# P1 moved by ScalarE into the PSUM bank of P2, and four sets of operand sums moved in the program

## The chip, the cores and the metric

The kernel runs on one core of one Trainium2 chip. The metric is the device time of one execution in microseconds (us). The core has a matrix engine (TensorE, PE in the profile; its weight loads are PEld), VectorE (DVE), ScalarE (ACT), GpSimd (POOL) and SyncE (SP). Each takes its instructions in the order in which they stand; an instruction that has to wait holds up all that stand behind it on the same engine. POOL and SP mostly issue DMA transfers here. Matrix products land in PSUM, eight banks of 128 partitions x 512 fp32, and are read from there by DVE and ACT.

## The reference

```python
# q, k, v: (4, 8, 768, 64); lam: (8,)
for b in range(12):                       # blocks of 64 positions
    intra = (q_b @ k_b.T * decay_mask) @ v_b
    out_b = intra + (q_b * lam ** (pos + 1)) @ kv_state
    kv_state = lam ** 64 * kv_state + (k_b * lam ** (63 - pos)).T @ v_b
x = out.transpose(0, 2, 1, 3).reshape(3072, 512)
h = x @ w_in                              # w_in: (512, 2048)
g = h - tanh(h)
return g @ w_out                          # w_out: (2048, 512)
```

A decayed linear attention gives 3072 tokens of 512 numbers; two dense layers with `h - tanh(h)` between them give the output. All in fp32.

## The kernel before

**Tiling.** The 768 positions are cut into six groups g of 128, so that a group of all four batches has 512 tokens. For each group the kernel computes the attention, then `up` (x @ w_in, in four strips u of 512 hidden units), then `down` (g @ w_out). Attention of group g + 1 is woven between the products of group g.

**Seven products for eight.** Each dense layer is done with the scheme of Strassen and Winograd: a product of 2 x 2 blocks needs seven block products P1 to P7 instead of eight, on sums of the blocks (S1 to S4 of one side, T1 to T4 of the other), and its results are sums of products. One result block is just P1 + P2. Sums of operands are DVE instructions: `sums_in(u)` (L279, four instructions of 128x512) makes S1, S2, S3, S4 of the first weights into `ws[u]`, `att_sums` (L569 to L572) those of the tokens, `sums_out(kt)` (L285) and `sums_fine(u)` (L303) those of the second weights, which POOL's DMAs store in DRAM (`factors`, `fine`). Some products are cut again by the same scheme: `down` products 3 to 7 (`down_twice`, L858), and for groups 2 to 5 `up` products 2 and 4 (`inner_steps`, L694), whose weight sums `inner_weights(u, ns)` (L667, four instructions of 128x128 per strip and product) makes and a DMA stores in `fine_in` (L668).

**Stages.** Group 0 does `up` plainly (`up_plain`, L917), while ACT and DVE round the weights (`weights`, `round_block`, L318 to L323). Its `down` (`down_first`, L947) runs over kt = 0 to 7, seven products of two matmuls each, into seven banks; between the rounds DVE makes sums for the rounds to come: `sums_late(kt + 1)` (L956, L957) must be ready before products 6 and 3 of round kt + 1. `first_results` (L963 to L972) adds the seven banks up on DVE. Then group 1 does `up` by the seven products (`up`, L610) in the order 2, 6, 5, 7, 1 of the next strip, 4, 3. Groups 2 to 5 follow.

**P1 + P2.** In `up` of group 1, ACT copies P1 out of bank y into SBUF (L633), P2 goes to bank w, DVE adds it to the copy (L635), ACT takes tanh of the sum and DVE subtracts. In `down` of groups 1 to 5, ACT copies P1 into the tile `q1` (L811), which later sums need too, and DVE adds P2's bank to it into `o11` (L827), which is stored.

**Buffers.** `ws[u]` hold the operand sums later, but first serve as room for second weights: `pair_tiles(kt)` puts the pairs kt = 2, 3, 6, 7 into `ws[3]` with `ws[2]` or `ws[1]`, the pairs 0, 1, 4, 5 into two buffers `wt`. The pool tag "sums" has four buffers, used in turn by `inner_weights`, `sums_twice` (L837, the sums for a product that is cut again) and `inner_tokens`. A buffer of `inner_weights` is free once its store to `fine_in` has landed. POOL's DMA queue also issues the loads of second weights for `down` (`piece`, wb, L764 to L770), each when a buffer of the ring of seven becomes free by a product of PE.

**Order.** Instructions of engines stand in an order that the framework's planner makes from the program's order and its own costs; those wrapped in `keep_in_program_order` (or `tied`, `hold`) keep the order of the program among themselves.

Of the kernel before, what the change touches and what calls it, by code (L numbers as in the profile page):

```python
# [15 lines left out]
AF = mybir.ActivationFunctionType  # L16
AL = mybir.AluOpType
# [7 lines left out]
def kernel(  # L25
# [32 lines left out]
    nc = tc.nc  # L58
# [8 lines left out]
    NU = DFF // 512  # L67
    KH = KO // 2
# [139 lines left out]
    ws = [wpool.tile([128, 3, 2, 256], F32, name=f"ws_{u}") for u in range(NU)]  # L208
# [13 lines left out]
    ready = {"loaded": 0, "done": 0}  # L222
# [42 lines left out]

    def pair_tiles(kt):

        if kt % 4 > 1:
            x, y = (ws[u].rearrange("p x k c -> p (x k) c") for u in (3, 4 - kt % 4))
            return x[:, ts(kt % 4 - 2, 2)], y[:, 0:6]  # L270
        wt = wst.tile([128, 8, 256], F32, name="wt", tag="w")
        return wt[:, 0:2], wt[:, 2:8]

# [51 lines left out]
    def bank(name, tag, bufs):  # L325
        return psum.tile([128, 512], F32, name=name, tag=tag, bufs=bufs)
# [251 lines left out]
    banks, hid, blks = {}, {}, {}  # L578

    def side(g, first):  # L580

        return "zw"[first] if g < GI else "wz"[first]

    def product_bank(key, n):

        if n == 1:
            banks[key, "y"] = bank("y", "yb" if key[0] == "up" and key[2] % 2 else "ya", 1)
        if n == 5 and key[1] >= GI:
            banks[key, "z"] = bank("z", "zw"[key[2] % 2], 1)
        elif n in (2, 5):  # L590
            banks[key, "zw"[n == 2]] = bank("zw"[n == 2], side(key[1], n == 2), 1)
        t = banks[key, {2: "w", 5: "z", 3: "z"}.get(n, "y")]
        return t.rearrange("q (m c) -> q m c", m=2), n in (1, 2, 5)

    def hidden(g, c):

# [4 lines left out]
    def up(g, u, n):  # L601
        a, bname = FACT[n]
        wt = {"A11": w1[u][:, 0:2, 0], "A12": w1[u][:, 2:4, 0], "S3": w1[u][:, 0:2, 1], "A22": w1[u][:, 2:4, 1],
              "S1": ws[u][:, 0], "S2": ws[u][:, 1], "S4": ws[u][:, 2]}[a]
        x = xt[g][bname] if bname != "B11" else xt[g, 0][:, 0:2]
        key = ("up", g, u)
        t, first = product_bank(key, n)
        for m in range(2):
            for kt in range(2):
                nc.tensor.matmul(out=t[:, m, :], lhsT=wt[:, kt, ts(m, 128)], rhs=x[:, kt, :],  # L610
                                 start=first and m == 0 and kt == 0, stop=kt == 1, skip_group_check=True)

        def dst(c):
            return hidden(g, c)[:, u]

        def finish(c, src):
            th = work.tile([128, 2, HB], F32, name="th", tag="th")
            nc.scalar.activation(th, src, AF.Tanh)  # L618
            nc.vector.tensor_tensor(dst(c), src, th, op=AL.subtract)  # L619

        y, z, w = (banks[key, x].rearrange("q (m c) -> q m c", m=2) if (key, x) in banks else None for x in "yzw")
        if g >= GI and n == 1:
            nc.vector.tensor_tensor(dst(11), dst(11), y, op=AL.add)  # L623
            finish(11, dst(11))
        elif g >= GI and n == 5:
            nc.scalar.activation(dst(22), z, AF.Copy)
        elif g >= GI and n == 7:
            nc.vector.tensor_tensor(dst(22), dst(22), y, op=AL.add)
            nc.vector.tensor_tensor(dst(21), dst(21), y, op=AL.add)
            finish(22, dst(22))  # L630
            finish(21, dst(21))
        elif n == 1:
            nc.scalar.activation(dst(11), y, AF.Copy)  # L633
        elif n == 2:
            nc.vector.tensor_tensor(dst(11), dst(11), w, op=AL.add)  # L635
            finish(11, dst(11))
        elif n == 6:
            nc.scalar.activation(dst(12), y, AF.Copy)  # L638
        elif n == 7:
            nc.scalar.activation(dst(22), y, AF.Copy)  # L640
            nc.vector.tensor_tensor(dst(22), dst(22), z, op=AL.add)  # L641
            finish(22, dst(22))
        elif n == 4:
            finish(21, y)
        elif n == 3:
            nc.vector.tensor_tensor(dst(12), dst(12), z, op=AL.add)
            finish(12, dst(12))

            nc.vector.tensor_tensor(dst("S1"), dst(12), dst(22), op=AL.add)
            nc.vector.tensor_tensor(dst(12), dst(11), dst(12), op=AL.subtract)  # L650
# [3 lines left out]
    INNER = (2, 4)  # L654
# [126 lines left out]
    def otile(name):  # L781
        return opool.tile([128, 512], F32, name=name, tag="o")

    res, low = {}, {}
# [7 lines left out]
    def down(g, n):  # L792

        if n in (1, 2):
            t, first = product_bank(("down", g), n)
        else:
            t, first = bank("plain", "w" if n == 7 else "z", 1).rearrange("q (m c) -> q m c", m=2), True
        a = hidden(g, HIDAT[FACT[n][0]])
        for u in range(NU):
            wb = piece(g, n, u)  # L800
            for m in range(2):
                for kt in range(2):
                    nc.tensor.matmul(out=t[:, m, :], lhsT=a[:, u, kt, ts(m, 128)], rhs=wb[:, kt, :],  # L803
                                     start=first and u == 0 and m == 0 and kt == 0, stop=u == NU - 1 and kt == 1,
                                     skip_group_check=True)
            if u + 1 < NU:
                yield
        t = t.rearrange("q m c -> q (m c)")
        if n == 1:
            res[g, 1] = otile("q1")  # L810
            nc.scalar.activation(res[g, 1], t, AF.Copy)  # L811
        elif n == 4:
            res[g, 4] = otile("q4")
            nc.scalar.activation(res[g, 4], t, AF.Copy)
        elif n == 7:
            o = otile("q7")
            nc.vector.tensor_tensor(res[g, 4], res[g, 4], t, op=AL.add)
            store(g, 21, res[g, 4])
            nc.vector.tensor_tensor(o, res[g, 5], t, op=AL.add)
            store(g, 22, o)  # L820
        elif n == 3:
            o = otile("q3")
            nc.vector.tensor_tensor(o, res[g, 5], t, op=AL.add)
            store(g, 12, o)
        else:
            o11 = late["pool"].tile([128, 512], F32, name="o11", tag="o11", bufs=1)
            tc.keep_in_program_order(nc.vector.tensor_tensor(o11, res[g, 1], t, op=AL.add))  # L827
            store(g, 11, o11)
        yield

# [58 lines left out]
    def steps(product, n):  # L889
        for _ in range(n):  # L890
            next(product)
# [130 lines left out]
    for u, cs, n0, n1, mid, more in turns:  # L1022
        turn = up_plain(u, cs)
        if n0:
            steps(turn, KI)
            run(mid)
            weights(ready["done"] + n0)
        every(turn)
        run(more)
        weights(ready["done"] + n1)  # L1030
        if cs[-1] == 22:
            sums_first(u)
            if u == 1:
                load_weights(NU * KI)
                load(2 * B)
                powers()
            if u == 2:
                sums_in(0)
    sums_out(0)
    sums_late(0)  # L1040
    att_out(1, P1, "att")
# [3 lines left out]
    for kt in range(KH):  # L1045
        down_first(kt, (1, 2, 5, 4, 7, 6, 3) if kt + 1 < KH else (1, 2, 6, 5, 7, 3, 4))
        if kt + 1 < KH:
            sums_late(kt + 1)
        if kt + 2 < KH:
            sums_out(kt + 2)  # L1050
        if kt in (0, 1, 3, 6):
            sums_fine((kt + 1) // 2)
        if 0 < kt and kt + 3 < KH:
            weights(ready["done"] + 2)
            load_weights(ready["done"] + WAHEAD)
        if kt == 5:
            att_sums(1)
    first_results()
    sums_in(1)
    early.close()  # L1060
    late["blk"] = ctx.enter_context(tc.tile_pool(name="blk", bufs=4))
    late["pool"] = ctx.enter_context(tc.tile_pool(name="late", bufs=1))
# [20 lines left out]
    for g in range(1, NG):  # L1083
        last = g == NG - 1
        for u in range(NU):
            for n in (2, 6, 5, 7, 1, 4, 3) if g < GI else (1, 7, 3) if u == 0 else (6, 5, 1, 7, 3) if u + 1 < NU else (
                    6, 5, 7, 1, 3):
                if n != 1:
                    up(g, u, n)
                elif u + 1 < NU:  # L1090
                    up(g, u + 1, 1)
                else:
                    if g == GI - 1:
                        inner_weights(u, INNER[:1])
                        pieces(g, u)
                    every(down(g, 1))
                if g == 1 and u < 2 and n == 5:
                    sums_in(u + 2)
            if g == GI - 1:
                inner_weights(u, INNER if u + 1 < NU else INNER[1:])  # L1100
            if g >= GI or u + 1 < NU:
                pieces(g, u)
        sums_twice(g, 4)
# [72 lines left out]
```

## Time and profile before

| what | value |
|---|---|
| median of three runs | 661.0 us (659.6 to 663.91) |
| the profiled execution: its own time, its span | 661.42 us, 659.6 us |
| TensorE clock granted over the span | 1.000 |
| PE, DVE busy | 645.3 us, 486.4 us |
| ACT, POOL busy | 216.7 us, 200.6 us |
| DMA mean | 196 GB/s |

The span reaches from the first to the last instruction; the execution's own time has some 1.8 us around it. In a line of the timeline the first number is the start in us from the span's start, the second how long it took (a row with x4 merges four instructions), then engine, line, operation, written <- read tiles, and in brackets the idle time of the engine before it with what ended it. A line of waits gives the total in us, how often, and the longest.

### The profile page before, as it was taken

What the parts mean: (1) busy time and instruction counts of PE and PEld (TensorE: products, weight loads), DVE (VectorE), ACT (ScalarE), POOL (GpSimd) and SP (SyncE); (2) the same over time, 40 slices, a digit from 0 to 9 for tenths busy, and PEclk for the clock granted to TensorE, in tenths of its full rate; (3) what the DMA queues carried; (4) which work ended last, traced back from release to release, by engine and by line L of the source; (5) the groups of instructions that cost most, each with busy time, mean ns of one, the idle gap of its engine ahead of it and who ended that gap; (6) DMA issues with size and microseconds to landing.
All of it is one profiled execution on the core that took longest, in us unless ns stands there. A gap on an engine that the chain in (4) does not pass through costs nothing.

```text
span 659.6 us, 14228 instructions
## 1 busy us (share of the span) xinstructions
PE 645.3 (98%) x5632; PEld 588.5 (89%) x5632; DVE 486.4 (74%) x869; ACT 216.7 (33%) x422; POOL 200.6 (30%) x349
## 2 busy tenths in 40 slices
PE   7899999999999999999999999999999999999997
PEld 6788988888788999988999988999988899988897
DVE  4576997997977876886877787787779687357563
ACT  4767773513231223232122243112223122334110
POOL 2000246773023554001445101355202354400250
PEclk9999999999999999999999999999999999999999
DMA  9988878999729676965578865587661677600481
GB/s 214 232 189 228 233 219 284 330 317 303 161 68 248 226 244 223 198 148 141 185 235 274 189 137 146 150 291 237 197 142 68 196 239 234 215 10 1 134 287 59
DMA packets 104818, 129.14 MB, mean 196 GB/s; under 512 B 63344, under 2 KB 80880, under 8 KB 104752
## 3 DMA queue, kind: packets, MB, share of 16 engines
q0 software_dynamic: 26400, 86.27, 41.2%
q1 hardware_dynamic: 78208, 41.96, 27.5%
q8 instruction: 45, 0.74, 0.5%
q14 instruction: 21, 0.17, 0.1%
q10 hardware_dynamic: 144, 0.00, 0.0%
HBM read 108.01 MB, written 20.19 MB: 194 GB/s over the span
## 4 chain that ended last, share of the span: by engine, by line
PE 79%; DVE 6%; DMA 6%; SPq 3%; issue 3%; ACT 1%; POOL 1%; DVEq 0%; POOLq 0%; ACTq 0%
PE y L610 15%; PE y L858 13%; PE zw L858 10%; PE z L610 9%; PE h L917 6%; PE y L803 5%; PE y L694 4%; PE w L803 4%; DMA k_blk<-in_k_dram 3%; PE z L694 2%; PE sp L448 2%; SPq L156 2%; PE acc L947 2%; DMA fine<-f 1%; PE op L484 1%
## 5 line engine op out<-in xcount | busy, mean ns | idle before, releaser
L767 POOL DMA_DIRECT2D wb<-fine x168 | 90.7, 540 | 156.7 <-PE y L858 53.0
L618 ACT ACTIVATE th<-g 128x512 f32<-128x512 f32 x76 | 47.5, 630 | 117.4 <-DVE g L623 48.9
L610 PE MATMUL y<-xt,w 128*128 128x256 f32 x320 | 74.0, 382 | 1.1 <-ACT g L638 1.1
L619 DVE TENSOR_TENSOR g<-g,th 128x512 f32<-128x512 f32 x76 | 52.4, 691 | 23.2 <-ACT th L618 22.8
L861 ACT ACTIVATE q<-y 128x128 f32<-128x128 f32 x96 | 26.7, 278 | 130.3 <-PE y L858 128.9
L610 PEld LDWEIGHTS y<-xt,w 128*128 128x128 f32 x320 | 59.8, 190 | 10.7 <-ACT g L638 2.7
L858 PE MATMUL y<-wb,g 128*128 128x128 f32 x456 | 60.2, 277 | 0.0
L917 PE MATMUL h<-xt,w 128*128 128x256 f32 x256 | 57.5, 381 | 2.4 <-DVE w L323 1.2
L917 PEld LDWEIGHTS h<-xt,w 128*128 128x128 f32 x256 | 47.8, 190 | 9.5 <-DVE ss L455 1.3
L770 POOL DMA_DIRECT2D wb<-factors x44 | 23.8, 543 | 106.2 <-PE y L803 70.2
L858 PEld LDWEIGHTS y<-wb,g 128*128 128x128 f32 x456 | 55.1, 192 | 0.6
L858 PE MATMUL zw<-wb,g 128*128 128x128 f32 x304 | 40.3, 275 | 0.2 <-DVE o L827 0.2
L610 PE MATMUL z<-xt,ws 128*128 128x256 f32 x160 | 37.9, 380 | 1.0 <-DVE g L641 1.0
L610 PE MATMUL y<-tt,ws 128*128 128x256 f32 x160 | 37.8, 379 | 0.0
L610 PE MATMUL z<-tt,ws 128*128 128x256 f32 x160 | 37.8, 379 | 0.0
L858 PEld LDWEIGHTS zw<-wb,g 128*128 128x128 f32 x304 | 37.0, 192 | 0.4 <-DVE o L827 0.4
L803 PE MATMUL y<-wb,g 128*128 128x256 f32 x160 | 35.4, 379 | 0.0
L803 PE MATMUL w<-wb,g 128*128 128x256 f32 x160 | 35.3, 379 | 0.0
L610 PEld LDWEIGHTS z<-xt,ws 128*128 128x128 f32 x160 | 30.3, 190 | 5.5 <-DVE g L641 1.4
L803 PEld LDWEIGHTS y<-wb,g 128*128 128x128 f32 x160 | 30.4, 190 | 4.1
L803 PEld LDWEIGHTS w<-wb,g 128*128 128x128 f32 x160 | 30.4, 190 | 4.1
L610 PEld LDWEIGHTS y<-tt,ws 128*128 128x128 f32 x160 | 30.1, 190 | 3.9
(188 smaller groups left out, 1293.8 us busy)
## 6 DMA issues: line engine op xcount, KB each, us to landing
wb<-fine POOLq DMA_DIRECT2D x168, 256.0 KB, 3.6
wb<-factors POOLq DMA_DIRECT2D x44, 256.0 KB, 4.4
wb<-fine_in POOLq DMA_DIRECT2D x24, 256.0 KB, 3.8
raw<-in_moe_w_out_dram POOLq DMA_DIRECT2D x10, 512.0 KB, 5.5
raw<-in_moe_w_in_dram SPq DMA_DIRECT2D x8, 512.0 KB, 6.1
raw<-in_moe_w_in_dram SPq DMA_DIRECT2D x16, 256.0 KB, 6.2
fine<-f POOLq DMA_DIRECT2D x16, 256.0 KB, 5.6
q_blk<-in_q_dram SPq DMA_DIRECT2D x32, 128.0 KB, 3.8
```

The source lines that it names most:

```text
L156: nc.sync.dma_start(out=x, in_=src[b, :, ts(g, BLK), :].rearrange("h s d -> s h d")))
L448: tied(True, nc.tensor.matmul(out=dst, lhsT=keys(p, j, late_), rhs=qt[ts(j, 64), p, rows], start=True, stop=True))
L610: nc.tensor.matmul(out=t[:, m, :], lhsT=wt[:, kt, ts(m, 128)], rhs=x[:, kt, :], start=first and m == 0 and kt == 0, stop=kt == 1, skip_gro ...
L618: nc.scalar.activation(th, src, AF.Tanh)
L619: nc.vector.tensor_tensor(dst(c), src, th, op=AL.subtract)
L694: nc.tensor.matmul(out=dst[:, ts(u, 128)], lhsT=a, rhs=b, start=x in (1, 2, 5) and u == 0, stop=True, skip_group_check=True)
L767: nc.gpsimd.dma_start(out=t.rearrange("p m c -> p (m c)"), in_=fine[TWICE.index(n_), SUB.index(x_)].rearrange("p u c -> p (u c)"))
L770: nc.gpsimd.dma_start(out=t, in_=factors[XAT[FACT[n_][1]]][:, 2 * x_:2 * x_ + 2, :])
L803: nc.tensor.matmul(out=t[:, m, :], lhsT=a[:, u, kt, ts(m, 128)], rhs=wb[:, kt, :], start=first and u == 0 and m == 0 and kt == 0, stop=u = ...
L858: nc.tensor.matmul(out=dst, lhsT=a[:, u, :], rhs=wb[:, ts(u, 128)], start=x in (1, 2) and u == 0, stop=u == NU - 1, skip_group_check=True)
L861: nc.scalar.activation(keep, dst, AF.Copy)
L917: tied(u == 0, nc.tensor.matmul(out=hm[c][:, m, :], lhsT=w1[u][:, i, a, ts(m, 128)], rhs=xt[0, t][:, i, :], start=m == 0 and i == 0, stop= ...
```

## The change

P1 of `up` in group 1, and P1 of `down` in groups 1 to 5, is copied by ACT from its bank into the bank of P2 (`begin_second`); the first matmul of P2 no longer starts that bank anew, so its products add to P1 there. DVE's two adds (L635, L827) are gone; `o11` is copied out of the bank by ACT. Besides, `sums_in(0)` goes from the third strip of group 0's `up` to round 4 of `down_first`, `att_sums(1)` from round 5 to round 4, `sums_in(1)` from behind `first_results` to round 6; the last pair of second weights is rounded in round 5 instead of 4, lies in a `wt` buffer, and pair 3 uses `ws[0]` instead of `ws[1]`. The `inner_weights` of product 4 for strips 0 to 2 go from the ends of their strips to strip 3, ahead of `down(1, 1)` in the program.

```diff
     def pair_tiles(kt):
-        if kt % 4 > 1:
-            x, y = (ws[u].rearrange("p x k c -> p (x k) c") for u in (3, 4 - kt % 4))
-            return x[:, ts(kt % 4 - 2, 2)], y[:, 0:6]
+        if kt in (2, 3, 6):
+            x, y = (ws[u].rearrange("p x k c -> p (x k) c") for u in (3, 0 if kt == 3 else 2))
+            return x[:, ts(kt % 2, 2)], y[:, 0:6]
...
-        elif n in (2, 5):
-            banks[key, "zw"[n == 2]] = bank("zw"[n == 2], side(key[1], n == 2), 1)
+        elif n == 5:
+            banks[key, "z"] = bank("z", side(key[1], False), 1)
         t = banks[key, {2: "w", 5: "z", 3: "z"}.get(n, "y")]
-        return t.rearrange("q (m c) -> q m c", m=2), n in (1, 2, 5)
+        return t.rearrange("q (m c) -> q m c", m=2), n in (1, 5)
+
+    def begin_second(key):
+        banks[key, "w"] = bank("w", side(key[1], True), 1)
+        nc.scalar.activation(banks[key, "w"], banks[key, "y"], AF.Copy)
...
         elif n == 1:
-            nc.scalar.activation(dst(11), y, AF.Copy)
+            begin_second(key)
         elif n == 2:
-            nc.vector.tensor_tensor(dst(11), dst(11), w, op=AL.add)
-            finish(11, dst(11))
+            finish(11, w)
...
             res[g, 1] = otile("q1")
+            begin_second(("down", g))
             nc.scalar.activation(res[g, 1], t, AF.Copy)
...
-            tc.keep_in_program_order(nc.vector.tensor_tensor(o11, res[g, 1], t, op=AL.add))
+            nc.scalar.activation(o11, t, AF.Copy)
             store(g, 11, o11)
...
-            if u == 2:
-                sums_in(0)
...
+        if kt == 5:
+            weights(ready["done"] + 2)
         if kt + 2 < KH:
             sums_out(kt + 2)
         if kt in (0, 1, 3, 6):
             sums_fine((kt + 1) // 2)
-        if 0 < kt and kt + 3 < KH:
+        if 0 < kt < 4:
             weights(ready["done"] + 2)
             load_weights(ready["done"] + WAHEAD)
-        if kt == 5:
+        if kt == 4:
             att_sums(1)
+            sums_in(0)
+        if kt == 6:
+            sums_in(1)
     first_results()
-    sums_in(1)
...
                     if g == GI - 1:
-                        inner_weights(u, INNER[:1])
                         pieces(g, u)
+                        inner_weights(u, INNER[:1])
+                        for x in range(u):
+                            inner_weights(x, INNER[1:])
                     every(down(g, 1))
...
             if g == GI - 1:
-                inner_weights(u, INNER if u + 1 < NU else INNER[1:])
+                inner_weights(u, INNER[:1] if u + 1 < NU else INNER[1:])
```

More of the change, by code (lines that the diff above doesn't have):

```diff
@@ L1093 @@
                     if g == GI - 1:
+                        pieces(g, u)
                         inner_weights(u, INNER[:1])
-                        pieces(g, u)
+                        for x in range(u):
+                            inner_weights(x, INNER[1:])
                     every(down(g, 1))
```

## The prediction

> **What bounds it.** I read the page's busy times first, then the waits of PE by length, then the timeline of PE and DVE where the change touches them, last POOL's timeline and the landings of `fine_in`.
>
> ```profile
> span 659.6 us, 14228 instructions
> ...
> PE 645.3 (98%) x5632; PEld 588.5 (89%) x5632; DVE 486.4 (74%) x869; ACT 216.7 (33%) x422; POOL 200.6 (30%) x349
> ```
>
> PE is busy 98% at a granted clock of 1.000. No PE work is removed, so a gain can come only out of PE's waits:
>
> ```profile
> PE h L917 <- DVE ss L455: 1.2, 1, 1.2
> PE y L610 <- ACT g L638: 1.1, 1, 1.1
> PE z L610 <- DVE g L641: 1.0, 1, 1.0
> PE acc L947 <- DVE s L956: 0.7, 2, 0.4
> PE sp L448 <- DVE kt L359: 0.6, 1, 0.6
> ```
>
> Together 4.6 us, all before 177 us. DVE (74%) can become the bound locally, so I follow its order against the moments at which PE wants its results. All times are in the clock of before; the order of each engine is that of the changed kernel's program.
>
> ```profile
> 76.58 0.69 DVE L279 TENSOR_TENSOR ws<-w 128x512 f32<-128x512 f32 x1
> ...
> 84.28 1.95 DVE L455 TENSOR_TENSOR ss<-sp,mask 128x384 f32<-128x384 f32 x4
> ...
> 137.85 0.69 DVE L569 TENSOR_TENSOR tt<-xt,xt 128x512 f32<-128x512 f32 x1
> ...
> 144.39 0.68 DVE L963 TENSOR_TENSOR o<-q,acc 128x512 f32<-128x512 f32 x1
> ...
> 149.16 0.68 DVE L279 TENSOR_TENSOR ws<-w 128x512 f32<-128x512 f32 x1
> ```
>
> The reader is to see that DVE runs without a gap from 130 to 152 us: what is put ahead of a step there delays it by its whole length. Four L279 take 79.11 − 76.58 = 2.53 us.
>
> **Step 1, the front: −1.2.** `sums_in(0)` leaves 76.58. PE's matmul L917 at 84.89 waited 1.18 for the mask L455; DVE reaches that 2.5 earlier, so the 1.18 goes. Bounds: 0 to −1.2. Later, until 131, DVE waits some 1.5 for DMAs of `fine`, which may swallow the rest of its lead.
>
> **Step 2, rounds 6 and 7 of `down_first`: +2.3.** In DVE's order `att_sums` (140.38 − 137.85 = 2.53) and `sums_in(0)` (2.53) now stand ahead of the sums for round 6, and the last rounding pair (2.33 from 133.26 to 135.59) goes behind these. The sums for round 6 (L956, ended 136.0) end at 138.74; PE wants them at 137.62: +1.17. In round 7 the rounded weights come 0.2 and the sums of L956 0.95 late. Round 7 ends at 147.70 where it ended at 145.39. If DVE kept its lead of 2.5 to here, this is 0.
>
> **Step 3, start of group 1: +1.05 more.** PE's order is the first product of strip 1 (1.73, to 149.43), two matmuls of product 5 into bank z, then P2. Bank z is free after the third sum of `first_results`. With two `sums_in` ahead of it (5.05), L963 starts at 149.44 instead of 144.39; the third sum ends 2.27 later (146.66 − 144.39), at 151.7: PE waits 2.3. The 1.12 at L638 goes. ACT's copy of P1 into bank w (a copy of 128x512 takes 0.60 in L811's row) is done by 150.8, hidden behind the 2.3. Products 5, 2, 6 (5.2) follow; product 7, which began at 153.58, begins at 156.93: **+3.35** for steps 2 and 3.
>
> **Step 4, strips 1 and 2.** The waits 0.97 (L641) and 0.59 (L359) go with L635 and its place; 0.5 of new ones come at the same transposes. Front in all: 3.35 − 1.56 + 0.5 − 1.18 = **+1.1**, bounds −0.1 (DVE's lead holds, steps 2 and 3 lose only 2.1) and +2.3 (step 1 gives nothing).
>
> **Step 5, end of group 1: +4.65.** Let T = 212.79, the end of `down(1, 2)`.
>
> ```profile
> 209.49 0.28 DVE L667 TENSOR_TENSOR ws<-w 128x128 f32<-128x128 f32 x1
> ...
> 210.42 0.69 DVE L837 TENSOR_TENSOR s<-g 128x512 f32<-128x512 f32 x1
> ...
> 218.79 0.69 DVE L837 TENSOR_TENSOR g<-g,s 128x512 f32<-128x512 f32 x1 [1.56 <-PE zw L858]
> ...
> 226.32 0.68 DVE L837 TENSOR_TENSOR gS<-gS,s 128x512 f32<-128x512 f32 x1
> ```
>
> ```profile
> 210.80 0.76 POOL L668 DMA_DIRECT2D fine_in<-ws  x1 [0.56 <-DVE ws L667]
> ...
> 213.15 0.54 POOL L767 DMA_DIRECT2D wb<-fine  x1 [1.04 <-PE w L803]
> ```
>
> ```profile
> 218.59 1.06 PE L858 MATMUL y<-wb,s 128*128 128x128 f32 x8
> ...
> 221.27 1.06 PE L858 MATMUL zw<-wb,g 128*128 128x128 f32 x8
> ...
> 227.53 1.06 PE L858 MATMUL zw<-wb,gS 128*128 128x128 f32 x8
> ```
>
> PE wants the first s2 at T+5.80, `g<-g,s` at T+8.48 and `gS<-gS,s` at T+14.74. Where before had 4 `inner_weights` sums (0.23 each, 209.49 to 210.42), 20 now stand in a row: 16 x 0.2 = 3.3 more. All share four buffers with the s tiles of L837: strip 3's product 4 needs the landed store of strip 3's product 2; the first s tile that of strip 0, the second that of strip 1, then strip 2, strip 3. The stores stand in POOL's queue between `wb` loads that wait for matmuls (POOL at 213.15 sat 1.04 for PE, 0.36 behind its matmul). So stores are issued at T−0.81 and T−0.05, then, behind the load for the last matmul of `down(1, 2)`, at T+1.25 and T+2.0; then come the store of `o11` and the last one. I take 4.5 us to landing, the row of 210.80, nearest in time (DMA share 1.04 from 205 to 215); the quiet rows at 194 to 195 give 2.7, that at 200.2 gives 6.3. Then:
> - strip 3's sums: T+3.7 to 4.6; s1 to 5.35; s2 from 5.75 to 6.5: PE waits 0.7;
> - third sum (0.6), two L789 (2.3), s, s, gS (0.7, 0.65, 0.6; the last store, issued at T+4.7, has landed by 9.2), `g<-g,s` (0.7): done T+11.9, PE late by 3.4;
> - from there to the end of `gS<-gS,s` DVE took 227.0 − 219.5 = 7.5, without a gap: T+19.4 against T+14.74, **+4.65** in all.
>
> The same sum gives +2.8 at 2.7 and +7.5 at 6.3. With buffers that never wait, all ends 3.3 − 0.6 (L827 gone) later, less the slack of 1.56 and 0.53: +0.6.
>
> The Trainium skill, "DMA: Bandwidth & Descriptors", section "Anatomy of one DMA — SWDGE (gpsimd) path", gives a fixed 2.0 us and bytes over 436 GB/s: an estimate of 2.45 us for 192 KB. The quiet rows (2.5 to 2.9) agree, 4.5 and 6.3 do not; by the page the ring would cost 2.7 and the time be 664.6.
>
> **Step 6, the nine copies from bank to bank: −0.2.** The trace has no ACT write into PSUM; the nearest row is its copy from PSUM to SBUF, 0.60. In `down`, product 3 (1.73) lies between P1 and P2, in `up` of group 1 two products (3.45), so copy and ACT's start (0.2 to 0.25) are covered. Without cover: 9 x 0.85 = 7.7. The adds that go (0.6 to 0.68) freed DVE where it waits for PE, by 2.49 in the row of 322.40 of L837: worth 0 to 0.2. In groups 2 to 5 nothing else changes.
>
> **Sum.** Profiled execution 661.42 + 1.1 + 4.65 − 0.2 = 667.0; the median of the runs is 0.4 below it, so **666.6** against 661.0, +0.8%. About 1% (6.6 us) is what a measurement of this kernel can tell from no change; +1% is 667.6.
>
> **Rivals.**
> - *The ring does not bind* (0.20): stores land early enough (about 1 us, or POOL gets through its loads earlier) that DVE never stops. For it: DMA share is 0.36 from 215 on. Against: no store landed under 2.5. 661.0 + 1.1 + 0.6 − 0.2 = 662.5; not slower to a degree that could be told.
> - *The DMA queues are full* (0.15): the stores meet the loads of the next group's attention (share 1.04) and land after 6.3, as at 200.2: 661.0 + 1.1 + 7.5 − 0.2 = 669.4.
> - *ACT's copies become PE's waits* (0.05), because ACT is late (a tanh ahead of the copy) or writes PSUM slowly: up to 7.7 on top of the forecast, 674. It decides only from a copy of over 1.5 us in `down`; nothing in the rows speaks for that.
> - *Faster* (0.05): DVE keeps its lead through `down_first`, and buffers come free; only the stalls go: 661.0 − 1.18 − 1.12 − 0.97 − 0.59 = 657.1. It needs DVE to make up 2.1 in rounds 6 and 7 and the stores to land by T. Steps 2, 3 and 5 speak against it.
>
> The forecast has 0.55, for 664 to 669. **Range** 661.5 to 671.0: it leaves out the two rivals of 0.05 and the tails of the unknown landing. **Chances:** even all waits of PE gone (−4.6) is under 1%: faster 0.02. Slower by over 1% are a third of the forecast (0.18), the full queues and the slow copies: 0.38. Within 1%: 0.60.
>
> **What will show it.** Step 1: no wait of h on L455. Step 2: waits of `acc` on L961 (once L956), 1.2 and 0.95. Step 3: z waits some 2.3 for `first_results`, y none for L638's successor. Step 5: y and zw of the products cut again (L863) wait 3 to 5 in all for DVE's L842 at about 220 to 235, and DVE before it for landings of `fine_in`. Step 6: no wait of PE on ACT's L598. I am wrong if stores land quickly, if DVE keeps its lead through `down_first`, or if the loads that wait behind the late products of group 1 hold up PE again in group 2, which no step counts.

## The result, and the profile after

The changed kernel takes 669.06 us (median of four, 668.06 to 670.38); the kernel before took 660.82 beside it. The ratio is **1.0119** (95% interval 1.0080 to 1.0158): slower by about 8 us. The profiled execution has a span of 667.1 us, 7.5 more than before. First the head of its page, then the waits of PE by length (us in total, how often, the longest):

```profile
span 667.1 us, 14232 instructions
...
PE 648.0 (97%) x5632; PEld 589.8 (88%) x5632; DVE 482.1 (72%) x860; ACT 221.9 (33%) x432; POOL 199.8 (30%) x349
```

```profile
PE y L863 <- issue: 3.1, 1, 3.1
PE zw L863 <- DVE g L842: 2.4, 1, 2.4
PE z L615 <- DVE q L971: 2.1, 1, 2.1
PE acc L952 <- DVE s L961: 1.7, 2, 1.0
```

All four were named in the prediction; the waits for L455, L638 and L641 are gone, and no PE wait for the copy L598 is listed. The DVE timeline at the end of group 1 shows where the first two come from (start, duration, and in brackets the idle time before):

```profile
208.26 0.69 DVE L654 TENSOR_TENSOR g<-g,g 128x512 f32<-128x512 f32 x1
208.87 1.09 DVE L359 STREAM_TRANSPOSE kt<-k_blk 128x512 f32<-128x512 f32 x1
209.83 0.26 DVE L671 TENSOR_TENSOR ws<-w 128x128 f32<-128x128 f32 x1
...
217.09 0.29 DVE L671 TENSOR_TENSOR ws<-w 128x128 f32<-128x128 f32 x1 [3.47 <-DMA fine_in<-ws]
...
218.03 0.69 DVE L842 TENSOR_TENSOR s<-g 128x512 f32<-128x512 f32 x1
220.41 0.69 DVE L842 TENSOR_TENSOR s<-s,g 128x512 f32<-128x512 f32 x1 [1.70 <-DMA fine_in<-ws]
...
225.83 0.68 DVE L842 TENSOR_TENSOR g<-g,s 128x512 f32<-128x512 f32 x1
```

DVE makes 16 sums in a row, stands 3.47 us until the store of the first of them has landed, then 1.70 until the third has. POOL's timeline gives the issues, PE's what waited:

```profile
211.60 1.53 POOL L672 DMA_DIRECT2D fine_in<-ws  x2 [0.27 <-DVE w L671]
213.13 0.57 POOL L771 DMA_DIRECT2D wb<-fine  x1
213.69 1.50 POOL L672 DMA_DIRECT2D fine_in<-ws  x2
...
219.61 0.77 POOL L672 DMA_DIRECT2D fine_in<-ws  x1 [3.70 <-DVE s L842]
```

```profile
221.21 1.13 PE L863 MATMUL y<-wb,s 128*128 128x128 f32 x8 [3.07 <-issue]
...
226.56 2.08 PE L863 MATMUL zw<-wb,g 128*128 128x128 f32 x8 [2.44 <-DVE g L842]
228.43 1.79 PE L863 MATMUL y<-wb,g 128*128 128x128 f32 x8
230.06 1.06 PE L863 MATMUL y<-wb,gS 128*128 128x128 f32 x8
```

The store issued at 211.60 let DVE go on at 217.09, 5.5 us later; the one at 213.69 at 220.41, 6.7 later. The 3.07 put down to "issue" is the wait for the tile `s` that DVE began at 220.41: PE starts on it 0.80 after.

PE ends `down(1, 2)` at T = 212.16 (212.79 before) and begins the product `z<-xt,ws` of group 2's first strip at 283.89 (276.31 before): 71.73 us for a stretch that took 63.52, **+8.2**. It consists of 3.25 up to 221.21 (9.05 from T, 5.80 before), 2.67 to 226.56 (5.35 for 2.68), 1.71 to 230.06 (3.50 for 1.79) and 0.57 to 238.72, where a load of `wb` came late. The 1.71 is no wait: sixteen matmuls took twice their time. A table by stretch (us; busy time of PE, PEld, DVE, ACT and POOL with their instructions; granted clock, DMA share, GB/s):

```profile
221.00:226.00 5.00, 2.92 (x24) 2.75 (x24) 4.96 (x8) 0.56 (x2) 2.11 (x4) 1.00 0.82 215
226.00:230.06 4.06, 3.50 (x16) 3.50 (x17) 4.06 (x7) 0.00 (x0) 0.54 (x1) 0.58 0.29 100
```

After the two stalls the clock granted to PE falls to 0.58 for 4 us. Most of the 1.71 stands where a wait would have been:

```profile
233.35 0.68 DVE L842 TENSOR_TENSOR gS<-gS,s 128x512 f32<-128x512 f32 x1
```

```profile
234.53 1.06 PE L863 MATMUL zw<-wb,gS 128*128 128x128 f32 x8
```

DVE has no wait from 220.41 until this `gS<-gS,s`, which it ends at 234.03. At full clock PE would have wanted it at 232.82 (226.56 and the 6.26 that lay between the same products before). It came to it at 234.53. By this estimate the fall of the clock added about 0.5 us and not 1.7.

### The profile page after: what moved, and what is told of

Read it like the earlier page. It is cut to its first block, busy times and chain, and to the rows that moved or that the text cites. A ratio compares the mean times of both kernels' runs of the same rounds, so it can differ in the third digit from the quotient of the medians.

```text
span 667.1 us, 14232 instructions
## 1 busy us (share of the span) xinstructions
PE 648.0 (97%) x5632; PEld 589.8 (88%) x5632; DVE 482.1 (72%) x860; ACT 221.9 (33%) x432; POOL 199.8 (30%) x349
## 4 chain that ended last, share of the span: by engine, by line
PE 77%; issue 6%; DVE 5%; DMA 4%; POOL 3%; SPq 3%; ACT 1%; POOLq 0%; DVEq 0%; ACTq 0%
PE y L615 16%; PE y L863 11%; PE z L615 10%; PE zw L863 8%; PE h L922 7%; PE y L807 5%; PE w L807 5%; PE y L698 4%; PE z L698 2%; PE sp L448 2%; SPq L156 2%; POOL wb L771 1%; PE op L498 1%; PE op L484 1%; DMA out_dram<-q 1%
## 5 line engine op out<-in xcount | busy, mean ns | idle before, releaser
L623 ACT ACTIVATE th<-g 128x512 f32<-128x512 f32 x72 | 45.0, 630 | 104.2 <-DVE g L628 48.9
L624 DVE TENSOR_TENSOR g<-g,th 128x512 f32<-128x512 f32 x72 | 49.6, 691 | 23.3 <-ACT th L623 22.9
L615 PEld LDWEIGHTS z<-tt,ws 128*128 128x128 f32 x160 | 30.0, 190 | 6.4 <-DVE q L971 2.5
```

## The experiments

The theory was the prediction's step 5: late sums fill the ring of four buffers with tiles whose stores land late. The first rival: another part of the change costs the time. The table has, for each kernel, the ratio to the kernel before run beside it, T, and the stretch from T to the first such product of group 2 in its profiled execution. T itself scatters: three kernels with the same front and the same copies (changed, e1, e7) reach it at 212.16, 214.16 and 213.92. The traces show two reasons. At the transposes L364 near 61 us, ahead of all moved sums, these executions stood at 60.62, 62.91 and 60.86. And in e7 the clock fell at 149.7 us, which cost 1.7. The stretch is the sharper measure.

| kernel | ratio (95%) | T | stretch |
|---|---|---|---|
| before | | 212.79 | 63.52 |
| changed | 1.0119 (1.0080 to 1.0158) | 212.16 | 71.73 |
| e1 changed, `inner_weights` back | 1.0022 (1.0001 to 1.0043) | 214.16 | 63.98 |
| e2 before + `inner_weights` moved | 1.0005 (0.9994 to 1.0017) | 213.45 | 63.41 |
| e3 before + copies | 0.9976 (0.9965 to 0.9987) | 211.36 | 63.41 |
| e5 before + front's moves | 1.0004 (0.9990 to 1.0018) | 214.27 | 64.25 |
| e6 front's moves + `inner_weights` | 1.0125 (1.0107 to 1.0144) | 212.24 | 70.78 |
| e7 changed, `inner_weights` first | 1.0018 (1.0005 to 1.0031) | 213.92 | 63.41 |
| e8 changed, no late stores | 1.0047 (1.0032 to 1.0062) | 214.45 | 65.23 |
| e9 copies, `inner_weights`, `sums_in(0)` in round 1 | 0.9939 (0.9918 to 0.9959) | 209.37 | 63.41 |
| e10 copies + `inner_weights` | 0.9967 (0.9958 to 0.9976) | 211.15 | 63.74 |
| e11 copies + `sums_in(0)` in round 1 | 0.9954 (0.9942 to 0.9967) | 210.82 | 63.46 |
| e12 e1 with `sums_in(1)` behind `first_results` | 0.9980 (0.9970 to 0.9991) | 210.69 | 63.41 |

**Each part alone.** e1 puts the late sums back:

```diff
-                        pieces(g, u)
-                        inner_weights(u, INNER[:1])
-                        for x in range(u):
-                            inner_weights(x, INNER[1:])
+                        inner_weights(u, INNER[:1])
+                        pieces(g, u)
...
-                inner_weights(u, INNER[:1] if u + 1 < NU else INNER[1:])
+                inner_weights(u, INNER if u + 1 < NU else INNER[1:])
```

> The changed kernel with the sums of the second operands of product 4 (inner_weights, strips 0 to 2) back at the ends of their strips; copies of P1 and the other moves of sums stay. Theory (four buffers shared with the sums of down, each free only when a store has landed, hold up DVE and then PE at the end of group 1): the 8.2 us between T and the start of group 2's first strip go, 669.1 - 8.2 = 660.9, and no wait of PE for L842 in group 1. Rival (the copies into PSUM or the front's moves cost the time): 666 or more.

The long stretch went (63.98), and 1.0119 became 1.0022; 662.77 us is nearer to the theory than to the rival, and 1.9 over it. The move of `inner_weights` is necessary for the loss. e2 is the reverse edit on the kernel before:

> The kernel before with that move of inner_weights alone. Theory: 660.8 + 8 = 668 to 670, waits of PE at the end of group 1 as in the changed kernel. Rival (the move matters only together with the rest, whose P1 copies on ACT or earlier arrival at T cause the waits): under 664.

Here the theory, as it stood, failed: 1.0005, a stretch of 63.41. The same move in the program costs nothing by itself. DVE's timeline of e2 shows why:

```profile
204.30 0.28 DVE L667 TENSOR_TENSOR ws<-w,ws 128x128 f32<-128x128 f32 x1
205.61 0.69 DVE L619 TENSOR_TENSOR g<-y,th 128x512 f32<-128x512 f32 x1 [1.03 <-ACT th L618]
...
210.15 0.28 DVE L667 TENSOR_TENSOR ws<-w 128x128 f32<-128x128 f32 x1
...
219.46 0.69 DVE L837 TENSOR_TENSOR g<-g,s 128x512 f32<-128x512 f32 x1 [1.57 <-PE zw L858]
```

The 16 sums end at 204.6, ahead of the tanh subtractions and 9 us ahead of T, in a place where the changed kernel's DVE sits idle (4.67 us at 204.33); only strip 3's last four stand late, as before. The planner had put them elsewhere than in the changed kernel. So a second part of the change must have shifted them. e3 and e5 give the other two parts alone, as in the change's diff:

> The kernel before with P1 copied into the bank of P2 alone (no sums moved). Theory: the copies lie behind a product everywhere and cost PE nothing; the wait for L638 (1.1) and part of the one for L641 (1.0) go, as DVE's add is gone: 658.5 to 661. Rival (copies become waits of PE): 663 to 668.

> The kernel before with the moves of sums_in, att_sums and the last rounding pair alone (DVE adds P2 as before, inner_weights stay). Theory of the prediction's steps 1 to 3: waits of 1.0, 0.7 and 2.1 at acc and z come, 1.2 at h and 0.7 at acc go, the add L635 stands behind first_results on DVE: 661 to 663. Rival (DVE's earlier lead carries through, as the changed kernel reached T 0.6 us early): 659 to 660.5.

The copies gain (0.9976), which is step 6 and the end of the waits for L638: no wait of a PE matmul for L598, and L645 (L641 once) costs 1.2. The front alone takes 661.83, in the theory's range, but its ratio of 1.0004 can't be told from no change.

**Which part shifts the sums.** e6 is e5 with e2's edit:

> The moves of sums (sums_in, att_sums, rounding pair) and the move of inner_weights together, without the copies of P1. In its order the 16 sums stand behind the last transpose of k (L359) and behind L650, as in the changed kernel; with inner_weights moved alone they stood some 15 instructions earlier. Theory (the place in DVE's order, which the planner sets, decides, and the copies have no part): 667 to 670, PE waits for L837 at the end of group 1. Rival (the copies are needed for the loss): under 664.

The whole loss without a single copy into PSUM: 1.0125, stretch 70.78. In its DVE timeline the sums stand behind the transpose, and DVE waits for a landing as in the changed kernel:

```profile
208.34 0.69 DVE L650 TENSOR_TENSOR g<-g,g 128x512 f32<-128x512 f32 x1
208.94 1.10 DVE L359 STREAM_TRANSPOSE kt<-k_blk 128x512 f32<-128x512 f32 x1
209.89 0.28 DVE L667 TENSOR_TENSOR ws<-w 128x128 f32<-128x128 f32 x1
...
216.78 0.29 DVE L667 TENSOR_TENSOR ws<-w 128x128 f32<-128x128 f32 x1 [3.08 <-DMA fine_in<-ws]
```

```profile
222.70 2.07 PE L858 MATMUL zw<-wb,g 128*128 128x128 f32 x8 [5.38 <-DVE o L827]
```

PE's wait has another name here: the add L827, which the copies remove, now stands behind the held sums, and it must empty bank zw. In this gap the clock fell too (0.63 from 219 to 221). e7 tests the place with the smallest edit, all moves and copies kept:

```diff
-                        pieces(g, u)
                         inner_weights(u, INNER[:1])
                         for x in range(u):
                             inner_weights(x, INNER[1:])
+                        pieces(g, u)
```

> The changed kernel with the calls of inner_weights in strip 3 put ahead of pieces (which issues the transposes) instead of behind it; nothing else. In its order the 16 sums then stand ahead of the transposes and of the last two tanh subtractions. Theory (place in the order): the loss at the end of group 1 goes, 660 to 663, as with the sums put back (662.8). Rival (the loss comes from moving the sums at all: more stores late, DVE busier): 666 or more.

1.0018 and 63.41: the loss is gone. In its order the sums stand ahead of the last transposes and of the tanh subtractions:

```profile
203.71 0.28 DVE L671 TENSOR_TENSOR ws<-w,ws 128x128 f32<-128x128 f32 x1
203.91 1.13 DVE L359 STREAM_TRANSPOSE qt<-q_blk 128x512 f32<-128x512 f32 x1
...
206.08 0.69 DVE L624 TENSOR_TENSOR g<-y,th 128x512 f32<-128x512 f32 x1 [1.04 <-ACT th L623]
```

So the loss needs two things: `pieces`, with the transposes, ahead of `inner_weights` in the program, and the front's moves, with which the planner puts the last transpose of k behind L654 and the sums behind that. Why the planner does this for one front and not for the other was not traced.

**What the place costs.** e8 keeps the late place but takes the late stores away: the product 2 sums of strips 0 to 2 are stored in place of those that are left out.

```diff
-            nc.gpsimd.dma_start(out=fine_in[INNER.index(n)].rearrange("x p u c -> p u x c")[:, u], in_=t[:, 0:3])
+            for i, x in put:
+                nc.gpsimd.dma_start(out=fine_in[i].rearrange("x p u c -> p u x c")[:, x], in_=t[:, 0:3])
...
+    PUT = (((0, 0), (1, 0)), ((0, 1), (1, 1)), ((0, 2), (1, 2), (0, 3)), ((1, 3),))
...
-                inner_weights(u, INNER[:1] if u + 1 < NU else INNER[1:])
+                inner_weights(u, INNER[:1] if u + 1 < NU else INNER[1:], PUT[u])
```

> The changed kernel, DVE's sums in the same late place, but without the four stores behind them: in place of the product 4 sums of strips 0 to 2 and the product 2 sums of strip 3, the product 2 sums of earlier strips are stored, at the ends of those strips (the output is not the reference's: these operands of product 4 are left out). No buffer then waits for a late landing. Theory (landings hold up the ring of four buffers): DVE's 3.3 us of sums alone cost at most 0.6, 660 to 662.5, no idle DVE for fine_in. Rival (DVE's extra instructions at the late place alone make PE wait): 665 or more.

DVE runs through without a wait for `fine_in`, and what is left of PE's waits there is small:

```profile
211.15 1.10 DVE L359 STREAM_TRANSPOSE kt<-k_blk 128x512 f32<-128x512 f32 x1
...
222.66 0.68 DVE L843 TENSOR_TENSOR g<-g,s 128x512 f32<-128x512 f32 x1
...
230.17 0.68 DVE L843 TENSOR_TENSOR gS<-gS,s 128x512 f32<-128x512 f32 x1
```

```profile
223.39 1.16 PE L864 MATMUL zw<-wb,g 128*128 128x128 f32 x8 [0.29 <-DVE g L843]
...
230.91 1.16 PE L864 MATMUL zw<-wb,gS 128*128 128x128 f32 x8 [0.90 <-DVE gS L843]
```

The stretch is 65.23: 1.8 over e7's 63.41 is the price of DVE's work in the late place, 71.73 − 65.23 = 6.5 that of waiting for landings, with the clock's fall. The medians differ by less, 4.8 us (669.06 and 664.28), and e8's profiled execution was 2.3 later at T (214.45). The measured 664.28 lies between the two expectations; the ring holds the larger part of the loss, not all of it.

**The front, and a better version.** e12 takes e1 and puts `sums_in(1)` behind `first_results`:

> The changed kernel with inner_weights put back, and sums_in(1) behind first_results again; sums_in(0) and att_sums stay in round 4. Theory (sums ahead of first_results make z wait 2.1): that wait goes, some 1 of it comes back at L645 in strip 1 as with the copies alone: 660.5 to 661.5 against 662.8. Rival (the wait only moves to the next sums): 662.5 or more.

659.34 us, 0.9980 against 1.0022, more than expected: the wait of z for L971 (2.1) is gone, without the one at L645. `sums_in(1)` ahead of `first_results` costs about 2.8 us together with the copies, where PE's order has two matmuls of product 5 ahead of P2. That is more than the wait of 2.1. The interval of e1 is wide (1.4 us to either side), and the clock may have a part: two of e1's five executions have a mean clock of 0.997, none of e12's eleven is under 0.999, and in e7 the trace shows the fall right behind this wait (the last section has its rows). Alone (e5) PE waits there 0.5 for L963 and 0.5 for L638. e9 combines the copies, the move of `inner_weights` and `sums_in(0)` where DVE waited for `fine`; the last of these edits is

```diff
-            if u == 2:
-                sums_in(0)
...
+        if kt == 1:
+            sums_in(0)
         if kt in (0, 1, 3, 6):
             sums_fine((kt + 1) // 2)
```

> A version that may beat both: copies of P1 and the move of inner_weights (whose sums stand early in this order), and sums_in(0) alone moved, from the third strip of group 0 to round 1 of down_first, ahead of sums_fine(1), where DVE waits 2.3 for landings of fine. att_sums, sums_in(1) and the rounding pair stay. Theory: the wait of h for L455 (1.2) goes without new waits at acc and z: 656.5 to 658.5, under the 659.2 of the copies alone. Rival (the sums come back as waits in down_first): 659 to 661.

**0.9939** (0.9918 to 0.9959), 657.17 us: faster than both. Of its waits of PE those behind the start, and DVE in the former gap (2.29 us in the run with the copies alone):

```profile
PE acc L952 <- DVE s L961: 0.7, 2, 0.4
PE sp L448 <- DVE kt L359: 0.6, 1, 0.6
PE z L615 <- DVE g L645: 0.4, 1, 0.4
```

```profile
109.09 0.68 DVE L279 TENSOR_TENSOR ws<-w,ws 128x512 f32<-128x512 f32 x1
...
112.11 0.69 DVE L303 TENSOR_TENSOR f<-ws,ws 128x512 f32<-128x512 f32 x1 [0.52 <-DMA fine<-f]
```

Two more runs divide the gain: e10 without the edit of `sums_in(0)`, e11 without the move of `inner_weights`.

> The copies of P1 and the move of inner_weights, nothing of the front; in its order the 16 sums stand early. Theory: no loss at the end of group 1, and 0.8 us of sums less at the ends of strips 0 to 2, so that the wait for L645 (1.2 with the copies alone) shrinks: 658 to 659. Rival (the copies make the moved sums late, as in the changed kernel): 666.

> The copies of P1 and sums_in(0) in round 1 of down_first, inner_weights where they were. Theory: the wait for L455 goes (1.2) and little else: 657.5 to 658.5. Together with the run before it tells how the gain of the version with all three (0.9939) divides.

The copies give −0.24%, `sums_in(0)` in the gap another −0.22% (e11); `inner_weights` moved alone −0.09% on the copies (e10), which the intervals leave open; those of e3 and e11 overlap by a hair (0.9965 and 0.9967). All three together give −0.61%.

## Why the prediction was right or wrong

Direction and size came out: 666.6 was forecast, 669.06 measured, inside 661.5 to 671.0; "slower by over 1%", at 0.38, was not the likeliest of the three classes. In the profiled execution the front came out 1.7 below its term and the end of group 1 3.6 above; the two errors partly cancel, so the nearness of the total is in part luck.

- **Bound and order.** Following DVE's order against PE's wants found every long wait. What the prediction did not see: it treated the late place of the 16 sums as what the move does. It is what the planner did with this move and the front's moves together (e2 against e6 and e7). The forecast held because it read the changed kernel's order; from the diff alone step 5 would be as wrong for e2 as it was right here.
- **Steps 1 to 4, front +1.1.** The waits came as sized: at acc 1.02 and 0.67 (1.17 and 0.95 forecast), at z 2.08 (2.3):

```profile
135.73 1.99 PE L952 MATMUL acc<-ws,s 128*128 128x256 f32 x8 [1.02 <-DVE s L961]
...
140.32 1.13 PE L952 MATMUL acc<-wt,s 128*128 128x256 f32 x4 [0.67 <-DVE s L961]
...
148.71 1.13 PE L615 MATMUL z<-tt,ws 128*128 128x256 f32 x4 [2.08 <-DVE q L971]
```

  From strip 1's first product (144.74, −0.65) to product 7 (154.00, +0.42) the lag grew by 1.07; step 3 said 1.05. The front in all gave −0.6 in this execution, +1.4 in e1, +1.1 in e7. The mis-sized term is step 1's lead: PE stood before round 6 at 134.71 (135.73 − 1.02), 2.9 ahead of 137.62, where 1.2 was forecast. The waits at acc of 0.34 and 0.40, which it also saves, were on the list and not counted. Another 1.1 was there at the transposes of 60.62 (61.70 before), so the moves did not make it; e1, 1.2 late at that point, was only 0.9 ahead at round 6. From these transposes to T the kernel before took 151.09, the changed one 151.54, e1 151.25: without the start the front's term is +0.2 to +0.5. Step 1 also put DVE's waits for `fine` at some 1.5; in the trace of before they are 0.26, 1.43 and 1.66.
- **Step 5, +4.65; measured +8.2.** Mechanism as described: strip 3's sums from 217.09 (T+4.9, 3.7 forecast), the first s2 PE needs 3.07 late (0.7 forecast), `g<-g,s` ended at T+14.4 (11.9 forecast). The mis-sized term is the time to landing: 5.5 and 6.7 for the two stores that mattered, not 4.5. The larger one makes PE 2.2 later than forecast, and its issue at T+1.5 in place of T+1.25 another 0.3. With that the forecast's own bound, `gS<-gS,s`, ended at T+21.9 (19.4 forecast): 7.1 in place of 4.65. Two terms were missing: the clock after the stalls (0.5, see above) and the load behind (0.6), which the last sentence of the prediction had only named; 7.1, 0.5 and 0.6 make the 8.2. The rival with full DMA queues took 6.3 and +7.5; its step was the closer one, its total of 669.4 by the same luck with the front.
- **The rivals.** The ring that does not bind: no. (The DMA share of 0.36 that spoke for it held only from 215 to 220 in the trace of before; from 220 to 225 it was 0.83.) What that rival priced at 0.6, DVE's work without waits, is 1.8 in e8; the last transpose of k (0.95), which now stands late too, was left out of it. Copies as waits of PE: none of a matmul in any run; the copies are the part of the change that gains.
- **Step 6.** Worth more than the 0.2 counted. e3 gains 0.24%, 1.6 us, mostly the 1.12 at L638, which step 3 had counted in the front and found eaten by the moved sums.

**The price by the Trainium skill.** The Trainium skill, "DMA: Bandwidth & Descriptors", section "Anatomy of one DMA — SWDGE (gpsimd) path", gives by estimate 2.45 us for these 192 KB. The store at 219.61 landed after 2.5, with a DMA share of 0.30 meanwhile; the ones that held DVE took 5.5 and 6.7, with shares of 0.91 and 0.75. So that price holds here for a store with little traffic beside it, and not for those that mattered. That the traffic makes the difference is the likely reason; no run changed the traffic alone.

## What to carry to other kernels

Where a planner sets the order of an engine, a moved step has to be looked up in the built order: one and the same edit cost 0 or 8 us here (e2, e6), by whether the planner put 16 small sums ahead of the last steps of a stage or behind them. A ring of buffers that a store must leave first is priced by the landing time at that moment, and by everything else that takes its buffers from the same ring. A step is best moved into a gap that the trace shows (`sums_in(0)` in round 1), not ahead of work on an engine that has none.

## What was unexpected of the hardware

- After waits of 3.07 and 2.44 us, with 2.92 us of PE work in the 5 us between 221 and 226, the granted clock fell to 0.58 and eight 128x128 matmuls took 1.87 us start to start instead of 0.90. In e7 the clock fell behind a single wait of 2.07; the wait ahead of that, of 0.67, had ended 6 us earlier:

```profile
148.76 1.13 PE L615 MATMUL z<-tt,ws 128*128 128x256 f32 x4 [2.07 <-DVE q L971]
149.73 3.41 PE L615 MATMUL w<-xt,w 128*128 128x256 f32 x8
```

```profile
149.73:152.93 3.20, 3.20 (x10) 2.54 (x8) 1.56 (x3) 0.00 (x0) 2.54 (x4) 0.53 1.00 288
```

  The changed kernel and e1, with the same wait, kept 1.00 there in their profiled executions. Of e7's ten executions five have a mean clock of 0.996 or 0.997 (662.5 to 663.7 us), five of 1.000 (660.5 to 663.1). The Trainium skill, "TensorE: Matmul & The Clock Gate", section "What's actually happening", ties the lower clock to an idle window of about 3.4 us. No gap of the changed kernel at this place or of e7 was that long; a gap of 5.38 (e6) was. What decides below that length stays open.
- ACT's copy of 128x512 from one PSUM bank into another took 0.58 us at each of its nine places (L598), a little less than the 0.60 of the copy into SBUF, and no matmul waited for one in any kernel here (a weight load of PE did, 0.2 us, once in each of five kernels).
